# A new order of all steps of a one-core delta-rule and MLP kernel, and two of its last stores on another queue

## The chip, the cores and the metric

The kernel runs on one core of a Trainium2 chip. A core has five engines, each with its own queue of instructions that it takes strictly in order: TensorE (PE: matmuls, with the weight load PEld shown apart), VectorE (DVE), ScalarE (ACT), GpSimd (POOL) and SyncE (SP, which here only issues DMAs). The metric is the device time of one execution in microseconds. Before the change three runs gave 534.24, 536.07 and 537.71 us; the median is 536.07.

## The reference: what is computed

Two blocks in a row, all in 32-bit floats. The first is a delta-rule recurrence over 768 steps for 4 batches of 8 heads of width 48. Each head has a 48 x 48 state that starts at zero:

```python
k_n = k / (norm(k) + 1e-6)
for t in range(768):
    y[:, :, t] = q_t @ state
    v_old      = k_t @ state
    state     += beta_t * outer(k_t, v_t - v_old)
```

The eight heads' outputs of a token are put side by side, which gives x of 4 x 768 x 384. The second block works on each token:

```python
xn  = (x - mean) / sqrt(var + 1e-6) * g_ln
out = x + relu(xn @ w_ch1) @ w_ch2      # 384 -> 1536 -> 384
```

## The kernel before, in words

The 768 steps are cut into 12 chunks, c = 0 to 11, of C = 64 tokens. Inside a chunk the recurrence is solved with matrices; from chunk to chunk only the state is handed on. What one chunk goes through, with the names that the text uses:

- Loads of q, k and v (`load_raw`, `load_blocks`, `load_v`, all through `dma`, L407 to L411), and transposes into `kt` and `qt`.
- The gram matrix of the keys, G (`gram`, L843): 64 small matmuls of 48 x 64, a copy to `gsb` by ACT, and a store `gd` to DRAM by SP.
- The triangular inverse, `rows_inverse` (L874), called x0, x1, ... : SP loads the gram back as `gb` in another layout; ACT takes the root of its diagonal and DVE makes scales of it (`nrm_b`, `db_b`, L892 to L897); then DVE runs a chain of pairs, a multiply into `tmp` (L916) and a subtract from `xb` (L923), in which each pair needs the one before. The result goes to DRAM (`xd`) and comes back in yet another layout (`xt<-xd`, called xq in the steps' names). From x1 on one such inverse serves two chunks: x1 chunks 2 and 3, x2 chunks 4 and 5, and so on. The first two chunks have inverses of their own: chunk 0's `first_inverse`, and x0 with blocks of FB = 16 for chunk 1.
- `join`, which puts the blocks together on PE, and `queries`, the products P of queries and keys.
- `recur` (L1030), the recurrence itself: on PE the products with the old state (ks, qs), the solve (u), the output (y) and the state's update (s, L1114); on DVE the sums v (L1049) and `s_all` (L1124).
- The norm: statistics of x on DVE (L1148, L1149), `xln` (L1160), and a turn on PE (L1192) to `xnt`.
- `mlp(c)`: the two matmuls with relu between. Chunk 0 does them plainly (L1416, L1438); later chunks compute the second one by a scheme with 7 of 8 block products (`seven`, L1492), and from chunk 3 on the first one by a similar scheme (`fifteen`, L1283). Both replace matmuls by additions on DVE and POOL. The sums of the second one end on DVE and POOL (L1531).
- `put(c, g)` (L1455): the stores of the result, two DMAs for each half g of the chunk's tokens, four for a chunk, 48 in all.

**What sets the order.** The code does not issue instructions as it goes. Every call of `add` (L68) appends a *step* to a list: its engine, a function that issues its instructions, and the steps that it depends on. There are 3016 steps (a step of PE can hold 64 matmuls). At the end `Line.emit` (L90) plays them in the order of a long string of step numbers, `ORDER` (L131 to L254). The order is chosen once, offline; nothing is decided while the kernel runs. The costs, priorities and due times in the calls are for the search that made the string, and `emit` uses only one of them: a GpSimd step is made to wait for the newest DVE step before it that uses the port which both share. `in_this_order` (L25) ties the instructions of each engine to that order, the DMAs of SP's and ACT's queues too. So on each engine the order of the string is the order of execution, and between engines only the data dependencies count. The letter "f" in the string is a filler: one matmul of zeros into an unused part of bank `f_[0]` (`zeros`, L1590, two instructions in the profile), whose result nobody reads.

The steps that the text calls by number, so that they can be found in the string: 304 is the store of x0's result; 372 and 378 split weights into two halves on DVE (L598); 418 is a transpose and 442 the sum v of chunk 1; 447 is chunk 1's `s_all`; 457 its `xln`; 646 is the gram matrix G4; 861 and 920 are an output sum of the MLP of chunk 1 and v of chunk 3; 916 is the product P3; 2024 and 2036 are the stores of the gram matrices of chunks 10 and 11, which x5 reads; 2043 to 2046 are x5's four small scale steps; 1782 and 1800 are output sums of chunk 5's second matmul, 1812 a matmul that reuses the bank that 1800 reads; 3005, 3006, 3014 and 3015 are the last four stores.

Of the kernel before, what the change touches and what calls it, by code (L numbers as in the profile page):

```python
# [16 lines left out]
C = 64  # L17
# [114 lines left out]
53 9 54 8 47 0 10 76 52 1 11-12 5 13 57 35 39 4 79 55 48 59 61 36 58 49 66 37 80 56 38 43 62 40 75 6-7 65 71 86 257  # L132
89 63 85 96 90 41 91 24 18 97 42 81 44 98 2 23 64 73 26 99 15 21 92 87 82 69 83-84 14 88 33 100 50 402 105 101-102
74 93 104 94 30 95 72 17 106 20 19 124 107 103 108 118 70 109 16 125 77 110 226 119 111 27 29 32 31 112 126 128 120
f f f 133 127 123 130 325 121-122 67 78 129 404 238 113 215 326 114 131 134 406 115-116 132 22 234 f 135 117 316 216
141 136 34 137 147 144 140 209 403 145 138 411 142 139 143 146 407 148-149 214 222 68 151 150 228 210 264 240 157
265 211 154 262 155 25 153 232 315 28 227 156 212 266 229 162 313 152 248 159 f 163 414 158 230 165 164 260 160-161
314 166 51 168 244 167 263 174 170 259 220 169 261 239 173 180 176 241 327 171 175 172 181 409 45 177 183 246 217
245 410 182 178 184 328 179 250 258 413 f f 185 60 191 189 256 317 242 401 186-187 196 46 193 190 197 192 188 247
318 194 199 267 195 213 198 268 319 363 200-201 243 269 205 320 270-271 273 203 f 321 272 208 274 202 275-276 204  # L140
277 249 207 278 322 251 279-280 3 364 281 f f 329 282 206 283 224 284 638 337 285-286 323 339 287 331 324 330 340
288 332 650 342 289-290 370 338 333 469 344 291-292 235-236 341 293-294 369 295-296 334 297 347 335 298-300 252 223
336 348 301 405 231 302 343 225 408 218 f f f f f 361 303 237 304 352 254 353 412 345 640 362 253 652 346 354 477
415 f 435 349 233 365 350 359 475 434 255 219 351 367 309 366 308 360 437 368 f f 355 310 376 375 312 436 221 358 f
f f 438 311 399 356-357 306 382 575 416 307 439 642 305 470 577 641 474 576 473 476 579 578 639 371 417 440 373 381
581 372 377 767 374 580 614 379 378 583 418 387 380 442 419 584 388 766 478 587 479 420 480-481 582 482 485 585 769
588 394 484 400 486 421 487 586 488-489 393 654 490-491 385 615 492 637 771 493 422 383 591 768 644 494 764 651 495
389 423 589 649 496 592 497-498 424 499 590 656 500 772 501 643 502 770 503 763 595 504 428 505 426 773 506 395 507
593 390 425 508 427 596 509 429 510 441 511 433 512 431 645 432 616 430 397 599 513 1052 443 514 594 396 655 391 515
653 444 516 483 517 398 774 600 445 518 1054 908 601 907 446 448 447 519 1056 910 520 909 521 657 522 646 449 384  # L150
523 386 629 451 597 524 647 1055 525 452 392 526 450 648 527 453 1051 454 528 658 1064 1058 617 659 602 1066 598 660
603 455 912 765 458 456 529 618 459 530 619 531 1053 532 620 533 1057 621 534-535 604 661 665 605 536 460 662 606
537-538 663 607 630 608 539 457 609 540-541 664 610 542-544 775 545 631 546 461 547 776 465 548 622 902 467 466 611
623 913 462-463 900 624 464 468 625 666-667 778 668-670 550 626 672 777 1068 673 911 549 805 674-675 551 676-678 809
632 806 679 552 680 807 681 1158 682-683 633 613 811 808 1157 684 810 685 914 686 813 687 904 688-689 1159 690 815
1059 814 627 812 901 817 691 1526 905 553 1160 692 554 693 818 694 816 819 695 556 779 555 557-558 823 696 1528 820
697-698 559 471 824 699 821 829 560 832 700 562 915 830 561 1070 563 822 780 701 1063 1163 702 831 564 838 906 781
703 825 704-705 1530 706 839 784 707 1067 1164 634 1165 708 782 612 785 835 709 786 565 710 1525 787 840 836 711 841
788-789 842 791 833 843 1167 792 472 712 827 783 628 834 1156 713 916 671 714 1166 828 844 715 1162 826 793 855 569
903 716 848 567 837 717 849 1155 568 790 718 850 1069 566 856 719 794 1168 857 720 858 845 721 1169 859 722 851 1529  # L160
795 723 852-853 796 847 860 724 917 797 846 570 862 801 725 571 918 726 1532 798 727 802 728 1531 854 800 865 729
799 1527 866 730 804 873 731 803 732 1065 874 573 733 875 734 574 919 735 920 736 572 921 1170 867 922 861 1352 876
# [87 lines left out]
2907-2908 2930 2941 2909 2945 2942 2946 2967 2910 2943 2954 2947 2955 2948 2944 2956-2957 2933 2949 2958 2952 2934  # L250
2959 2968 2951 2960 2969 2935 2971 2961 2970 2972-2973 2962 2989 2981 2950 2974 2978 2975 2982 2953 2983 2990-2991
2963 2992 2984-2986 2993 2987 2976 2994 2988 2996 2995 2980 2997-2998 2979 2999-3001 3007 3002 3008 2977 3009 3003
3010 3004 3011-3012 3006 3013-3014 3005 3015
"""  # L254


# [1482 lines left out]
```

## Time and profile before

| | |
|---|---|
| runs | 534.24, 536.07, 537.71 us (median 536.07) |
| profiled execution | 533.75 us, span 532.0 us from first to last instruction |
| mean granted TensorE clock | 0.985 of full speed |
| instructions | 22724 |
| busy: PE, weight load | 497.6 us (94%), 451.9 us (85%) |
| busy: DVE, POOL, ACT | 366.4 us (69%), 281.3 us (53%), 207.9 us (39%) |
| moved by DMA | 54.56 MB, 181635 packets, most under 512 bytes |

The profile is of one execution. It gives the busy time of each engine, the same in 40 slices of the span (13.3 us each; a digit is the busy share in tenths, 9 means 90% or more), the granted clock of TensorE in the same slices, and the chain of work that ended last, followed back from the end. The trace behind it can be asked for windows (busy time of each engine in a stretch), for waits (what an engine waited for, by the line of the waiting instruction and the line of the one that released it), and for a timeline. Two instructions on one engine can overlap a little, as the start of the next is prepared while one ends.

### The profile page before, as it was taken

To read this page: it belongs to the slowest core of one execution; us is meant where nothing else is said; L and a number is where in the kernel's file an instruction comes from. 1 tells how busy PE (TensorE), PEld (TensorE's weight loads), DVE (VectorE), ACT (ScalarE), POOL (GpSimd) and SP (SyncE) were. 2 spreads that over 40 slices of the span, in tenths; PEclk is the share of its full clock that TensorE was granted. 3 is DMA by queue.
4 is the path that set the end of the run, shared out by engine and by line. 5 is a ranking of instruction groups with operands and counts; after the bars stand their busy time and mean duration, and the time that the engine had idled before them with its cause. 6 is when DMAs were issued, how large, how long until landed. Compare 5 with 4: busy or idle time off the path is not lost.

```text
span 532.0 us, 22724 instructions
## 1 busy us (share of the span) xinstructions
PE 497.6 (94%) x9942; PEld 451.9 (85%) x9942; DVE 366.4 (69%) x819; ACT 207.9 (39%) x451; POOL 281.3 (53%) x447
## 2 busy tenths in 40 slices
PE   5978798989989999999999999999999999999996
PEld 2766676758778888899999899999999999999996
DVE  3677748899996697994799982789985546244241
ACT  5677645412423332343342433442422623524130
POOL 6015574460573948757827617464266353554554
PEclk9789999999989999999999999999999999999999
DMA  9948798357635657156625157532435411212011
GB/s 174 289 73 194 178 207 160 78 111 139 119 58 120 150 115 123 34 141 154 100 65 97 21 135 198 116 70 33 101 74 104 91 31 37 56 40 53 1 30 31
DMA packets 181635, 54.56 MB, mean 103 GB/s; under 512 B 164888, under 2 KB 177312, under 8 KB 181536
## 3 DMA queue, kind: packets, MB, share of 16 engines
q1 hardware_dynamic: 168672, 40.30, 37.2%
q10 hardware_dynamic: 10656, 9.64, 6.6%
q0 software_dynamic: 2208, 3.17, 3.8%
q8 instruction: 78, 1.28, 1.0%
q14 instruction: 21, 0.17, 0.1%
HBM read 36.30 MB, written 16.78 MB: 100 GB/s over the span
## 4 chain that ended last, share of the span: by engine, by line
PE 67%; DVE 18%; issue 4%; ACT 2%; DMA 1%; POOL 1%; SPq 0%; ACTq 0%; DVEq 0%; POOLq 0%
PE f L1513 26%; PE f L1316 22%; DVE tmp L916 5%; PE f L1416 5%; DVE xb L923 4%; PE two L828 3%; PE by L1042 2%; PE two L1042 2%; PE by L1104 1%; PE two L1097 1%; DVE qt L923 1%; PE two L1114 1%; ACT xt L738 1%; DVE words L1488 1%; DVE st L1148 1%
## 5 line engine op out<-in xcount | busy, mean ns | idle before, releaser
L1513 PE MATMUL f<-w_sb,h_all 128*128 128x192 f32 x396 | 83.8, 331 | 1.8 <-issue 1.6
L1500 POOL TENSOR_TENSOR h_all<-h_all 128x256 f32<-128x256 f32 x99 | 73.9, 759 | 13.8 <-DVE tmp L916 6.3
L1513 PE MATMUL f<-words,h_all 128*128 128x192 f32 x396 | 80.0, 333 | 0.6 <-POOL h_all L1500 0.6
L1538 POOL TENSOR_TENSOR words<-h_all 128x128 f32<-128x128 f32 x66 | 30.3, 477 | 78.2 <-ACT h_all L1343 51.6
L1513 PEld LDWEIGHTS f<-words,h_all 128*128 128x128 f32 x396 | 66.0, 192 | 2.3 <-POOL h_all L1500 1.4
L1339 DVE TENSOR_TENSOR h_all<-f,h_all 128x512 f32<-128x512 f32 x72 | 48.8, 685 | 27.0 <-PE f L1316 22.0
L1513 PEld LDWEIGHTS f<-w_sb,h_all 128*128 128x128 f32 x396 | 65.7, 191 | 1.5 <-ACT words L1544 0.3
L916 DVE TENSOR_TENSOR tmp<-xb,gb 128x31 f32<-128x31 f32 (+19 forms) x139 | 60.2, 433 | 4.4 <-POOL xb L903 1.5
L923 DVE TENSOR_TENSOR xb<-xb,tmp 128x31 f32<-128x31 f32 (+19 forms) x139 | 55.5, 399 | 2.9
L410 POOL DMA_DIRECT2D tb<-in_k_dram x64 | 41.7, 655 | 20.5 <-DVE xb L923 9.3
L1416 PE MATMUL f<-xnt,w_sb 128*128 128x256 f32 x216 | 51.2, 384 | 0.0
L1334 ACT COPY h_all<-f 128x512 f32<-128x512 f32 x45 | 25.9, 586 | 61.6 <-PE f L1316 42.0
L1343 ACT ACTIVATE h_all<-h_all 128x512 f32<-128x512 f32 x54 | 32.9, 627 | 35.9 <-DVE h_all L1339 35.8
L1416 PEld LDWEIGHTS f<-xnt,w_sb 128*128 128x128 f32 x216 | 39.9, 190 | 7.3 <-issue 1.8
L1316 PE MATMUL f<-xnt,w_sb 128*128 128x128 f32 x288 | 41.1, 278 | 0.0
L1316 PE MATMUL f<-x_new,w_sb 128*128 128x128 f32 x288 | 40.7, 277 | 0.0
L1316 PEld LDWEIGHTS f<-x_new,w_sb 128*128 128x128 f32 x288 | 37.1, 191 | 0.4
L1316 PEld LDWEIGHTS f<-xnt,w_sb 128*128 128x128 f32 x288 | 36.7, 191 | 0.6
L611 POOL TENSOR_TENSOR w_sb<-words 128x768 uint32<-128x768 uint32 (+1 forms) x11 | 15.6, 1425 | 35.9 <-ACT xt L738 23.2
L1531 DVE TENSOR_TENSOR o<-f,x 128x192 f32<-128x192 f32 x33 | 11.3, 353 | 31.6 <-PE f L1513 29.1
L1142 ACT COPY x<-by 128x384 f32<-128x384 f32 x23 | 10.4, 480 | 43.8 <-DVE o L1531 28.1
L1425 ACT ACTIVATE h_all<-f 128x256 f32<-128x256 f32 x36 | 13.3, 380 | 36.0 <-PE f L1416 35.9
(252 smaller groups left out, 989.6 us busy)
## 6 DMA issues: line engine op xcount, KB each, us to landing
words<-in_moe_w_ch_dram ACTq DMA_DIRECT2D x20, 384.0 KB, 5.3
gd<-gsb SPq DMA_DIRECT2D x11, 512.0 KB, 3.1
v<-in_v_dram SPq DMA_DIRECT2D x24, 192.0 KB, 4.3
out_dram<-o SPq DMA_DIRECT2D x48, 96.0 KB, 2.3
kr<-in_k_dram SPq DMA_DIRECT2D x46, 96.0 KB, 3.7
xld<-xlt SPq DMA_DIRECT2D x9, 384.0 KB, 2.9
xnt<-xld SPq DMA_DIRECT2D x36, 96.0 KB, 2.8
tb<-in_q_dram SPq DMA_DIRECT2D x40, 64.0 KB, 3.2
```

The source lines that it names most:

```text
L410: add(eng, cost, lambda: QUEUE[eng].dma_start(out=out_, in_=in_), r, w, bulk=n * ns / 16e3, np=n, **kw)
L916: lambda j=j, n=n, w=w, t=t: nc.vector.tensor_tensor(out=t, in0=xv[:, 0:n, j : j + 1].to_broadcast([128, n, w]), in1=gv[:, j : j + 1, j + ...
L923: "DVE", dve(n * w), lambda t=t, rest=rest: nc.vector.tensor_tensor(out=rest, in0=rest, in1=t, op=ALU.subtract),
L1042: nc.tensor.matmul(dst[half(e), hp, j], src[drows(hp), (e if n else key_half(c, hp, e)) * GP + j], s_all[drows(hp), e, j], start=(n == 0 o ...
L1316: nc.tensor.matmul(wide(p[:, f : f + 128]), w[:, f : f + 128], r, start=start and i == 0, stop=True, skip_group_check=True)
L1334: add("ACT", act(512), lambda: nc.scalar.copy(o, p), pk, ok)
L1339: add("DVE", dve(512), lambda: nc.vector.tensor_tensor(out=o, in0=x, in1=y, op=op), [*xk_, *yk], ok)
L1343: add("ACT", act(512), lambda: nc.scalar.activation(o, o, ACTF.Relu, scale=scale), [], ok)
L1416: nc.tensor.matmul(p[:, 0:TOK], w1_sb[:, t, f * 128 : (f + 1) * 128], xnt[:, t], start=(t == 0), stop=(t == KC - 1))
L1500: add(eng, cost, lambda: e.tensor_tensor(out=out_, in0=x, in1=y, op=op), r, w, port=2 if eng == "Pool" else 1, pr=-2)
L1513: lambda f=f, t=start and f == order[0]: nc.tensor.matmul(p[:, 0:D2], lhs(f), rhs[:, f], start=t, stop=(f == order[-1]), skip_group_check=True
L1538: lambda f=f + i: e.tensor_tensor(out=s3[f], in0=one(0, 0)[0](f), in1=one(1, 0)[0](f), op=ALU.subtract),
```

## The change

Two edits. First, the string `ORDER` is replaced as a whole. The set of steps and their dependencies are the same; the new string comes from a new search, in which the time that each transfer takes was varied at random many times. It holds 15 fillers where the old one has 21. Seventy-three of the 3016 steps keep their place in the list; half of them move by 14 places or less, the farthest by 747. Second, in `put`, for the last chunk (c = 11), the store of the second pair of batches (e = 1) is issued from ACT's queue instead of SP's. These are the steps 3006 and 3015, one for each half g of the tokens.

```diff
 ORDER = """
-53 9 54 8 47 0 10 76 52 1 11-12 5 13 57 35 39 4 79 55 48 59 61 36 58 49 66 37 80 56 38 43 62 40 75 6-7 65 71 86 257
...
-3010 3004 3011-3012 3006 3013-3014 3005 3015
...
+2993-2994 2996-2997 2995 2998-3002 2979-2980 2988 3007-3013 3004 3003 3015 3006 3005 3014
 """
...
     def put(c, g):
         for e in range(2):
             dma(
-                "SP", out[2 * e + g, c * C : (c + 1) * C, :], os_[g][half(e)], C, 105, o_keys(g), [("out", c, g, e)], pr=-5
+                "ACT" if e and c == NCH - 1 else "SP", out[2 * e + g, c * C : (c + 1) * C, :], os_[g][half(e)], C, 105, o_keys(g), [("out", c, g, e)], pr=-5
             )
```

The new string is nine lines shorter, so every line of the kernel behind it has a number that is lower by nine after the change. What it does to the places that the text speaks of:

- At the start, three large fill matmuls stand behind the first transposes instead of ahead of them, and the loads of beta's rows come first on POOL. DVE takes x0's chain in among chunk 0's inverse. SP issues the store 304 directly behind a gram store.
- Steps 372, 378, 418 and 442, which DVE ran just ahead of x1's chain, stand inside it, and 861 and 920 move in among x1 and x2.
- ACT's root for x1 stands ahead of two relus of chunk 0's MLP.
- Steps 2043 to 2046 stand ahead of the sums 1782 and 1800 on DVE; on SP both gram stores 2024 and 2036 and x5's gb loads stand ahead of loads that were ahead of them.
- At the end SP's queue holds 3005 and then 3014, ACT's holds 3015 and then 3006.

## The prediction

> **What bounds the kernel now.** I read the page first: shares of engines, the span in slices, the chain that ended last.
>
> ```profile
> PE 497.6 (94%) x9942; PEld 451.9 (85%) x9942; DVE 366.4 (69%) x819; ACT 207.9 (39%) x451; POOL 281.3 (53%) x447
> ...
> PE   5978798989989999999999999999999999999996
> ...
> DVE  3677748899996697994799982789985546244241
> ...
> PEclk9789999999989999999999999999999999999999
> ...
> PE 67%; DVE 18%; issue 4%; ACT 2%; DMA 1%; POOL 1%; SPq 0%; ACTq 0%; DVEq 0%; POOLq 0%
> ```
>
> TensorE is busy for 94% of the span, so an order of the same instructions can win no more than its idle time: 532.0 − 497.6 = 34.4 us, and the slices put nearly all of that in the first half. The windows say how much is where, and what stands beside it (columns: span, then busy of PE, weight load, DVE, ACT, POOL, granted clock, DMA share, GB/s).
>
> ```profile
> 100.00:150.00 50.00, 44.76 (x936) 34.84 (x924) 47.69 (x103) 14.74 (x39) 22.00 (x32) 1.00 0.64 123
> 150.00:200.00 50.00, 47.39 (x1295) 42.16 (x1296) 38.39 (x84) 16.74 (x43) 30.59 (x40) 0.97 0.52 109
> 300.00:350.00 50.00, 49.94 (x1037) 48.13 (x1036) 34.36 (x79) 19.11 (x39) 22.77 (x40) 1.00 0.58 133
> ...
> 150.60:154.70 4.10, 4.06 (x72) 3.94 (x73) 3.93 (x12) 1.23 (x4) 1.49 (x3) 0.58 0.13 16
> ```
>
> From 100 to 150 us PE is idle 5.2 us while DVE is busy 47.7 of 50: DVE sets the pace there. It works off two inverses, x1 (DVE 78.79 to 121.35) and x2 (122.85 to 161.6), nearly without a gap, and what PE waits for stands behind them in DVE's queue. From 300 us PE has next to nothing to win and everything to lose. The chain's 18% of DVE is this first part. The waits of PE name the single stalls (total, times, longest):
>
> ```profile
> PE f L648 <- DMA u<-in_beta_dram: 2.6, 1, 2.6
> PE by L1192 <- DVE xln L1160: 2.6, 1, 2.6
> PE two L828 <- DVE s_all L1124: 2.2, 1, 2.2
> ```
>
> **The change part by part.** For each step I summed, with the durations of this execution, the work that stands ahead of it on its own engine in the old and in the new order. The difference says how much earlier or later its engine reaches it. It cannot say when its input is there, and that is where I chose.
>
> *Fillers.* 21 become 15.
>
> ```profile
> L1591 PE MATMUL f<-u 128*128 128x256 f32 x42 | 12.7, 432 | 0.0
> ```
>
> Two matmuls each: 12.7 / 21 = 0.60 us, six fewer is 3.6 us of PE busy time. They stand in the first 75 us, where PE idles 5.6 us of 0–13, 6.1 of 27–53 and 5.9 of 53–100, so I count 0 (bounds −3.6, if PE never waits where they stood, and +1.7, below). After PE had been busy 2.41 us of the 4.60 before 150.6, the clock was granted at half for 3.41 us (the 0.58 row above); one such stretch costs PE 3.41 / 2 = 1.7 us. The Trainium skill ("TensorE: Matmul & The Clock Gate", Part 1: The HAM clock gate) says that the array falls to half rate only after at least one idle window of about 3.4 us; no wait of PE here is longer than 2.6 us, and the clock fell all the same, so the trace is stricter than that rule; by the rule the missing fillers could cost nothing.
>
> *Start and x1.* The inverse x0 is moved forward among the first chunk's inverse on DVE. Its result's store, step 304, is what x1 waits for in the end (through the loads of xq, the gram store's queue and gb).
>
> ```profile
> 58.77 1.88 SPq L410 DMA_DIRECT2D beta_b<-in_beta_dram  x2
> 60.75 0.53 SPq L410 DMA_DIRECT2D xd<-xb  x1
> ...
> 65.38 6.05 SPq L410 DMA_DIRECT2D xt<-xd  x8
> 71.47 1.51 SPq L410 DMA_DIRECT2D gb<-gd  x2
> ```
>
> SP issued it 1.9 us after x0's last DVE step (58.83 to 60.75), behind two beta loads. In the new order these stand elsewhere, and from the store to the last gb load SP holds as much as before (12.2 against 12.4 us). So x1's chain starts 1.9 us earlier (bounds 0 and −6.2, the latter being SP's work less ahead of step 304). But four DVE steps that lay in DVE's idle time before x1 (8.3 us of it between 65 and 79 us) are now inside the chain: 372 (1.86), 378 (0.55), 418 (0.71), 442 (0.92), 4.04 us. With 861 and 920 also moved in, x1 and x2 together hold 88.3 us of DVE work against 83.0. At x2's end DVE is thus 5.3 − 1.9 = 3.4 us late before waits are counted; the gap between them (121.35 to 122.85) takes 1.3 of it, leaving 2.1.
>
> What PE sees of this, with PE's own work ahead (fillers off) against DVE's: G4 (646) needs chunk 1's state sum (447), which has 3.05 us more DVE work ahead while PE has 0.7 less: a new stall, 3.2 us. The L1192 wait grows by 0.3. The join of chunk 2 loses 0.7. The 2.2 us wait of P3 (916) goes, since PE has 2.27 us more work ahead of it and 4.9 when the fillers are left out; with it the idle time that came before the half clock at 151, 1.7 us. Sum: 3.2 + 0.3 − 0.7 − 2.2 − 1.7 = **−1.1 us** (bounds −6, when x1 starts 6 us earlier and the 3.2 goes, and +5.3, when it starts no earlier and all of DVE's extra work is paid).
>
> Late next, once these stalls go, is the recurrence at 205–235 us: DVE has 4 to 7 us more ahead of its steps there, but 12.8 us idle to take it, so 0. Without that cover it would be those 4 to 7 us, which I keep in the upper end.
>
> *Inverse x5 and chunk 5's sums.* In the new order the four small DVE steps that wait for x5's gb loads (2043 to 2046, 0.9 us) stand ahead of the sums 1782 and 1800 of the second matmul; before, they ran at 339.86 and the sums at 328.2. DVE takes its queue in order, and PE's step 1812 needs 1800 to have emptied its bank.
>
> ```profile
> 327.91 0.36 DVE L1531 TENSOR_TENSOR o<-f,words 128x192 f32<-128x192 f32 x1 [6.45 <-PE f L1513]
> ...
> 332.01 1.98 SPq L410 DMA_DIRECT2D gb<-gd  x2
> ...
> 335.20 1.09 SPq L410 DMA_DIRECT2D gb<-gd  x2
> ```
>
> The loads were issued late since the gram store 2024 stood behind xt loads until 327.85 although its data were there at 315.4. In the new order both gram stores stand ahead of these, the other one's data (320.26) being last; SP then holds 4.6 us to the end of the gb issues, 324.9, and from the last issue to the norm it took 3.3 us before (336.29 to 339.56): gb at 328.2, so the sums run about 1 us late. If instead SP is late as before, the loads gain only the 2.7 us that SP holds less between store and loads: 337.1 and 0.9 on top, 9.5 us late with everything of PE behind. I take **+2.0 us** (bounds 0 and +9.5), near the lower end, since the gram's data are long there.
>
> *The last stores.*
>
> ```profile
> 526.93 2.56 SPq L410 DMA_DIRECT2D out_dram<-o  x4
> 527.35 0.36 DVE L1531 TENSOR_TENSOR o<-f,o 128x192 f32<-128x192 f32 x1 [1.40 <-PE f L1513]
> ```
>
> SP issues all four: step 3006 at 526.93, 3014 at 527.74 (it waits for the last sum, done at 527.71), 3005 at 528.26, 3015 from 528.90 to 529.49; the last lands at 532.0. In the new order SP has 3005 and 3014, so it ends at 528.2, and ACT, idle there, has 3015 and then 3006. ACT takes its queue in order, so 3006, whose data are there at 526.91, stands behind 3015 and its wait for 527.71: with 0.37 to 0.50 us for one issue on ACT (its loads between 4 and 21 us) it ends at about 528.7. **−0.7 us** (bounds −1.3, if the landing follows SP's end, and 0, when transfers share engines so that the last one lands no earlier). The Trainium skill ("DMA: Bandwidth & Descriptors", Issuing engines are not separate DMA queues) says that issuing from several engines saves only the sequencer's time to issue; that time is what this term counts.
>
> Sum: 0 − 1.1 + 2.0 − 0.7 = +0.2 us on the profiled execution's 533.75 (span 532.0 and 1.75 around it), 533.9. That execution lies 2.3 us under the median of the runs, 536.07; on the median I forecast **536.3 us**.
>
> **Rivals.**
>
> *Slower: x5's norm blocks DVE at 328 us.* One mechanism: DVE's queue stands at step 2043 until gb lands, PE at 1812. Each microsecond that gb lands after 328.4 costs one, as PE has 0.06 us idle in that window. It passes 1% when the sums run about 7 us late (2.0 + 5.2), at 335.5. Full price 9.5 − 2.0 more than my sum: **543.8 us**. For it: some 20 loads and stores share SP from 316 to 336 us. Against: the stores are first there now.
>
> *Slower: x1 starts no earlier.* The four DVE steps are paid in full in a stretch that DVE paces, +5.3 instead of −1.1: **542.7 us**. For it: 47.69 of 50; against: 8.3 us of DVE's idle time before 79 us that an earlier chain can use.
>
> *Faster: the chain gets its 6.2 us.* If step 304 leaves by as much earlier as SP's queue allows, G4's new stall and the L1192 wait go, −6 instead of −1.1, 531.4 us, and the fillers' 3.6 us may come off the start's own path: **527.8 us**. For it: 29 us of PE's idle time lie before 300 us. Against: x0's own DVE chain must be that early.
>
> *The order moves nothing on the path.* PE's stalls only change places; the stores alone count: 536.07 − 0.7 = **535.4 us**.
>
> *Half clock.* If, with fewer fillers, two or three more stretches of 3.41 us at half clock follow, 1.7 us each: +3.4 to +5.1, about **540.5 us**.
>
> **How the numbers follow.** One per cent, 5.4 us, is about what a measurement of this kernel tells from no change. Chances: my sum 0.30, the order moving nothing 0.10, half clock 0.10 (three with the time within 1%, mostly), x5's block 0.13, x1 no earlier 0.10, the faster rival 0.27. The bounds of the terms spread each by some 3 us. Faster than 530.7: 0.27 — most of the faster rival and the low tail of my sum. Slower than 541.4: 0.28, from the two slower rivals and the high tails. Within: 0.45. The range 527 to 545 takes in both x5's full price and most of the faster rival; my sum's own range is 531 to 541.5.
>
> **What would show it.** Right: L1192 and L828 waits of PE change as told (2.2 gone, a new one at L828 behind s_all near 100 us); no 0.58 clock near 151; x1's first step at 76.9 instead of 78.8; the wait of DVE before the norm L893 near 328 about 1 to 3 us; last four stores in two queues, issued 0.7 us sooner after the last matmul. Wrong: PE's idle time from 300 us over 5 us, a wait of several microseconds on gb there, or x1's first step before 74 or after 80 us. What would make it wrong is a producer that moves later than the work ahead of it tells, most of all a DMA, since transfers' landing times under a new neighbourhood are in no sum of mine.

## The result, and the profile after

The changed kernel takes 554.51 us (median of four runs, 552.69 to 558.17); the kernel before took 536.89 us beside it (four runs). The ratio is 1.034 with a 95% interval of 1.0269 to 1.0411: 18 us slower. The forecast was 536.3 us, no change, with a range of 527 to 545; the result lies outside it.

The page of the changed kernel, of an execution of 552.69 us with a span of 550.9 us and a mean clock of 0.965 (engines; the slices of PE, DVE and the clock; the chain that ended last):

```profile
PE 500.1 (91%) x9930; PEld 456.0 (83%) x9930; DVE 375.8 (68%) x819; ACT 207.0 (38%) x451; POOL 284.2 (52%) x447
...
PE   3887699989899887699999999999999999999996
...
DVE  3567769899985489996499984698955436344141
...
PEclk9797799999899997989999999999999999999999
...
PE 60%; DVE 14%; DMA 4%; SPq 4%; issue 2%; ACT 1%; POOL 1%; DVEq 0%; ACTq 0%; POOLq 0%
```

PE's idle time, span less busy, grew from 34.4 to 50.8 us; its busy time grew by 2.5 us although six fillers are gone. Together that is the 18.9 us of the span. The clock's row has sevens in its slices 2, 4, 5 and 16 (13.8 us each, so 14 to 28, 41 to 69 and 207 to 220 us) and eights in 11 and 18. From the 19th on it is full, as before: the second half lost nothing.

To place the loss I took, in both traces, the moment at which PE had done the same amount of its work (without fillers). The new kernel is 5.7 us behind at 70 us of the old one's time, 4.5 at 196, 11.7 at 208, 16.6 at 220, 18.2 at 231, and then 17 to 20 to the end. Between the first two the lag falls to about 3 us near 110 and rises to 7 or 8 near 140; as the two orders differ, each figure holds to some 2 us. So there are two places: **the start**, and **the stretch from 200 to 240 us**, where some 14 us go. The windows of the second one, first of the kernel before, then of the changed one (span, busy of PE, weight load, DVE, ACT, POOL, clock, DMA share, GB/s):

```profile
205.00:210.00 5.00, 5.00 (x33) 5.00 (x32) 2.57 (x5) 1.95 (x5) 3.57 (x5) 1.00 0.70 112
230.00:235.00 5.00, 5.00 (x98) 4.75 (x98) 4.48 (x8) 1.89 (x4) 3.64 (x7) 1.00 0.85 264
```

```profile
205.00:210.00 5.00, 0.00 (x0) 0.00 (x0) 4.59 (x14) 0.10 (x1) 0.00 (x0) 0.85 0.17 30
210.00:215.00 5.00, 4.48 (x72) 4.39 (x73) 4.72 (x10) 0.80 (x1) 2.80 (x4) 0.50 0.03 7
...
230.00:235.00 5.00, 1.37 (x48) 1.27 (x40) 4.97 (x6) 0.80 (x2) 4.11 (x5) 0.74 0.07 10
235.00:240.00 5.00, 5.00 (x24) 5.00 (x24) 4.38 (x11) 0.89 (x4) 2.65 (x3) 0.58 0.05 7
...
100.00:150.00 50.00, 44.61 (x890) 34.02 (x890) 45.84 (x95) 16.94 (x40) 22.41 (x30) 0.97 0.50 99
150.00:200.00 50.00, 47.63 (x1188) 41.99 (x1188) 33.83 (x75) 18.28 (x47) 24.39 (x35) 1.00 0.61 123
300.00:350.00 50.00, 48.46 (x968) 46.80 (x968) 36.60 (x76) 15.81 (x33) 32.14 (x51) 1.00 0.63 124
```

Twice PE stands still, and twice the clock is then granted at about half for some 7 us. The three wide windows, in which the prediction looked for gains and losses, moved by 1.5 us of PE's busy time at most. PE's waits in the changed kernel say what it stood for (total, times, longest; line numbers are nine lower than before):

```profile
PE f L639 <- POOL ident L421: 8.3, 1, 8.3
PE two L1088 <- DVE v L1040: 6.3, 1, 6.3
PE f L1504 <- DVE o L1522: 4.7, 2, 3.6
PE f L1582 <- DVE u L1074: 4.5, 1, 4.5
...
PE by L1183 <- DVE xln L1151: 2.4, 3, 1.5
```

The 8.3 for `ident` is not lost as such: before, PE filled that time with its fill matmuls, and its first transposes of keys started at 7.26 us, where they start at 8.60 now.

The 6.3 is the recurrence of chunk 4 (u4), which waits for its sum v, step 1175 on DVE. That step runs at 209.52 us; before, it ran at 183.5. Its two inputs come later too: PE's product ks4 ends at 194.8 instead of 182.5, and POOL's step 1161 moved from 171.5 to 199.7. POOL's timeline shows what happened to 1161 (start, duration, line, operation; in brackets the idle time ahead):

```profile
180.67 1.14 POOL L1522 TENSOR_TENSOR o<-o,words 128x192 f32<-128x192 f32 x2
194.74 1.29 POOL L894 COPY xb<-db_b 128x32 f32<-128x32 f32 x1 [12.92 <-DVE db_b L888]
195.96 0.45 POOL L1529 TENSOR_TENSOR words<-h_all 128x128 f32<-128x128 f32 x1
196.35 0.66 POOL L401 DMA_DIRECT2D tb<-in_k_dram  x1
197.02 0.88 POOL L1529 TENSOR_TENSOR words<-h_all 128x128 f32<-128x128 f32 x2
197.84 1.27 POOL L1267 TENSOR_TENSOR w_more<-w_more,w_sb 128x512 f32<-128x512 f32 x1
199.05 0.66 POOL L401 DMA_DIRECT2D tb<-in_k_dram  x1
199.72 1.49 POOL L682 TENSOR_TENSOR v<-v,kpair 128x768 f32<-128x768 f32 x1
201.15 0.87 POOL L1529 TENSOR_TENSOR words<-h_all 128x128 f32<-128x128 f32 x2
201.98 0.72 POOL L1491 TENSOR_TENSOR h_all<-h_all 128x256 f32<-128x256 f32 x1
202.66 1.26 POOL L1267 TENSOR_TENSOR pt<-pt,w_sb 128x512 f32<-128x512 f32 x1
```

The copy at 194.74 is step 1086, which puts the scales of x3's diagonal into `xb`. It waits for x3's norm. In the new order 1161 (the L682 row) and others stand behind it, fifteen steps with 12 us of work by the durations of before, that stood ahead of it there (950, 955, 980 to 985, 1161, 1350, 1525, 1531, 1532, 1537, 1540). Ten of them had their inputs by 182.6 us; the loads for 1161 had all been issued by 155.2. POOL takes its queue in order, so it idles 12.92 us and then does most of this work in one run. That run meets x3's chain on DVE, of which step 1090 is one. In the kernel before, then in the changed one, where the last row is v of chunk 4:

```profile
192.70 0.22 DVE L916 TENSOR_TENSOR tmp<-xb,gb 128x60 f32<-128x60 f32 x1
```

```profile
196.49 0.47 DVE L914 TENSOR_TENSOR xb<-xb,tmp 128x31 f32<-128x31 f32 x1
196.99 7.01 DVE L907 TENSOR_TENSOR tmp<-xb,gb 128x60 f32<-128x60 f32 x1
204.04 0.22 DVE L914 TENSOR_TENSOR xb<-xb,tmp 128x60 f32<-128x60 f32 x1
...
209.52 0.95 DVE L1040 TENSOR_TENSOR v<-v,two 128x768 f32<-128x768 f32 x1
```

Step 1090, a multiply of 128 x 60 that takes 0.22 us before, takes 7.01 us: it begins with POOL's run of nine instructions at 197.02 and ends with it, at 204.00 against 203.92. What stands behind it on DVE, v of chunk 4 among it, is late by that much. When v starts, 1161 has been done for 8 us (201.21) and DVE has had no idle time just ahead: in the end v waits for its place in DVE's queue, behind x3's steps, and not for 1161.

### The profile page after: what moved, and what is told of

Its sections match the earlier page's. It is cut to its first block, busy times and chain, and to the rows that moved or that the text cites. A ratio compares the mean times of both kernels' runs of the same rounds, so it can differ in the third digit from the quotient of the medians.

```text
span 550.9 us, 22698 instructions
## 1 busy us (share of the span) xinstructions
PE 500.1 (91%) x9930; PEld 456.0 (83%) x9930; DVE 375.8 (68%) x819; ACT 207.0 (38%) x451; POOL 284.2 (52%) x447
## 4 chain that ended last, share of the span: by engine, by line
PE 60%; DVE 14%; DMA 4%; SPq 4%; issue 2%; ACT 1%; POOL 1%; DVEq 0%; ACTq 0%; POOLq 0%
PE f L1504 21%; PE f L1307 19%; PE f L1407 7%; DVE tmp L907 5%; SPq L401 4%; DVE xb L914 3%; PE two L819 2%; PE two L1088 2%; PE by L1095 2%; PE two L1033 1%; PE by L1033 1%; DMA xld<-xlt 1%; PE two L1105 1%; DMA xnt<-xld 1%; DVE qt L914 1%
## 5 line engine op out<-in xcount | busy, mean ns | idle before, releaser
L1504 PE MATMUL f<-w_sb,h_all 128*128 128x192 f32 x396 | 85.7, 335 | 7.8 <-DVE o L1522 3.6
L907 DVE TENSOR_TENSOR tmp<-xb,gb 128x31 f32<-128x31 f32 (+19 forms) x139 | 69.1, 497 | 4.5 <-POOL xb L894 1.2
L914 DVE TENSOR_TENSOR xb<-xb,tmp 128x31 f32<-128x31 f32 (+19 forms) x139 | 60.9, 438 | 3.0
L1407 PEld LDWEIGHTS f<-xnt,w_sb 128*128 128x128 f32 x216 | 41.1, 195 | 9.5 <-issue 2.1
L1522 DVE TENSOR_TENSOR o<-f,x 128x192 f32<-128x192 f32 x33 | 11.5, 350 | 43.5 <-PE f L1504 38.5
L1307 PE MATMUL f<-xnt,w_sb 128*128 128x128 f32 x288 | 39.9, 279 | 0.0
L1307 PEld LDWEIGHTS f<-xnt,w_sb 128*128 128x128 f32 x288 | 36.9, 194 | 0.3
L1504 PE MATMUL f<-w_sb,words 128*128 128x192 f32 x132 | 27.7, 329 | 1.1 <-DVE o L1522 1.1
L1416 ACT ACTIVATE h_all<-f 128x256 f32<-128x256 f32 x36 | 13.3, 382 | 31.5 <-PE f L1407 30.7
```

What stands on the lines that cost most here:

```text
L907: lambda j=j, n=n, w=w, t=t: nc.vector.tensor_tensor(out=t, in0=xv[:, 0:n, j : j + 1].to_broadcast([128, n, w]), in1=gv[:, j : j + 1, j + ...
L914: "DVE", dve(n * w), lambda t=t, rest=rest: nc.vector.tensor_tensor(out=rest, in0=rest, in1=t, op=ALU.subtract),
L1307: nc.tensor.matmul(wide(p[:, f : f + 128]), w[:, f : f + 128], r, start=start and i == 0, stop=True, skip_group_check=True)
L1407: nc.tensor.matmul(p[:, 0:TOK], w1_sb[:, t, f * 128 : (f + 1) * 128], xnt[:, t], start=(t == 0), stop=(t == KC - 1))
L1416: lambda hk=hk, p=p: nc.scalar.activation(h_all[:, hk] if c <= LNPE else h_all[:, hk].rearrange("p (g i b) -> p i g b", g=2, b=BK), p[:, 0 ...
L1504: lambda f=f, t=start and f == order[0]: nc.tensor.matmul(p[:, 0:D2], lhs(f), rhs[:, f], start=t, stop=(f == order[-1]), skip_group_check=True
```

## The experiments

All experiments change only the string `ORDER` (and the stores, where said), so the work is the whole of the reference's. Intervals are 95%; a percentage times the some 536 us of the kernel before gives the microseconds.

**Which part of the order (h1, h2, h3).** Two hybrids, cut at step 1060, the gram matrix G6 (near 150 us).

```diff
 ORDER = """
-(old string)
+(new string up to 1060; then the steps left, in the old string's order)
```

> The new order up to and with step 1060 (gram G6, 173.0 us in the new profile, 169.7 in the old), then all steps left over in the old order, stores on SP. Theory 'region': of the 18 us, 3 to 4 are lost before G6 and 14 behind it, between 200 and 240 us, by the new order of POOL and DVE around x3 and chunk 4. Then this kernel is 2 to 5 us slower than the old one, about 540, c4's sum v (1175) is no more than 5 us later than in the old profile (183.5), and DVE's step 1090 takes its 0.2 us. Theory 'start': the new start makes x3's gram loads late, and everything behind follows from that; then this one is 12 to 18 us slower, about 552. Theory 'spread': the loss is all over; then about 545.

Measured: 543.32 against 536.86 us, 1.0114 (1.0075 to 1.0153), +6.1 us.

```diff
 ORDER = """
-(old string)
+(old string up to 1060; then the steps left, in the new string's order)
```

> The old order up to and with step 1060, then all steps left over in the new order, last stores in two queues. Theory 'region': 12 to 15 us slower than the old kernel, about 550, with POOL idle for about 10 us ahead of x3's copy (1086), one DVE step of x3 that takes several us, and PE waiting 4 us or more at u4 (1176) for v. Theory 'start': within 4 us of the old kernel, about 538. Theory 'spread': about 545.

Measured: 548.82 us, 1.0232 (1.0178 to 1.0285), +12.5 us. The two add up to 18.6 us, the whole loss being 18.2: two separate causes, and the larger one lies behind G6. In h2's trace POOL's run holds x3's step of 128 x 87 for 4.82 us, and PE waits 5.3 us for v of chunk 4, as in the full change.

A third hybrid takes the new order only to step 361, s of chunk 0.

```diff
 ORDER = """
-(old string)
+(new string up to 361; then the steps left, in the old string's order)
```

> The new order only up to and with step 361 (chunk 0's state, 67.0 us in the new profile, 60.0 in the old), then all steps left over in the old order, stores on SP. The new order up to G6 (173 us) with the old rest cost 1.1%, 6 us. Theory 'start': chunk 0's u and state come 7 us later, since DVE runs x0's chain among chunk 0's inverse, and x1, x2 and what follows inherit it: 4 to 7 us slower than the old kernel (0.8 to 1.3%). Rival 'middle': DVE makes up for the start while it waits for x1, and the loss is made by the order between 67 and 173 us: under 2 us slower (under 0.4%).

Measured: 541.03 against 534.84 us, 1.0107 (1.0061 to 1.0152), +5.7 us. The new start with the old rest thus costs as much as the whole first part (h1). It is not quite the start of the change, though: x1's norm comes at 87.7 us in h3, at 76.2 in h1 and at 77.4 in the changed kernel. That the first part is lost in the first 70 us is read from the lag of 5.7 us there; what x1 and x2, which the prediction argued over, add to it or give back, these runs do not tell apart.

**POOL's queue behind 1086 (e2, e8a, e10, e6).** In the changed kernel four of the delayed POOL steps go back ahead of 1086.

```diff
-888 892 ... 943 980 1531 981 983 950 1540 1161 984 982 986 1087 955 1088
+888 980 950 1161 955 892 ... 943 1531 981 983 1540 984 982 986 1087 1088
```

> The new order with four POOL steps (980, 950, 1161, 955; 4.5 us of work), whose inputs are there by 180 us, taken from behind x3's copy 1086 to ahead of it (behind 888), into POOL's 12.9 us of waiting. Nothing moves on DVE. Theory 'run on POOL holds DVE': in the new profile DVE's step 1090 took 7.01 us (0.22 elsewhere) and ended when POOL's run of additions (195.96 to 203.92) ended; with 4.5 us less in the run it takes about 2.5, v of chunk 4 (1175) comes 4.5 us earlier, PE's wait of 6.3 us at u4 falls to 2 or less, and the kernel gains 4 to 8 us (with some half clock), about 548. Rival 'place in DVE's queue': v is late since 25 steps of x3 stand ahead of it, not for 1090's length; then 1090 stays above 5 us, and the kernel gains under 2 us, about 553. Third: DVE's step 1090 waits for something else that the profile does not show (its length unchanged at 7).

Measured: 549.52 against 536.86 us, 1.0226 (1.0186 to 1.0267): 12.1 us over the kernel before where the change has 18.2, so four moved steps bring 6 back. The step that took 7.01 us takes 0.53.

Then twelve steps.

```diff
-888 892 ... 963 926 ... 959 938 ... 943 980 1531 981 983 950 1540 1161 984 982 986 1087 955 1088
+888 1525 1531 1532 1161 980 950 955 1537 1540 892 ... 963 983 926 ... 959 981 982 938 ... 943 984 986 1087 1088
```

> The new order with twelve POOL steps taken from behind x3's copy 1086 to ahead of it, as they stood in the old order: 1161, 980, 950, 955, 983, 981, 982 and the transfers 1525, 1531, 1532, 1537, 1540, 9.6 us of POOL's time by the old profile. POOL waited 12.9 us ahead of 1086 in the new profile with all of them behind it. Only POOL's order changes. Theory 'POOL's queue': DVE's steps 1090 (7.01) and 1130 (4.27) fall under 1.5 us each, v of chunk 4 comes some 6 us earlier, PE's waits at u4 (6.3) and at 1042 (3.6) fall under 2 us, and 9 to 13 us come back: 542 to 546. Rival 'order on DVE and PE': v (1175) still stands behind 25 steps of x3 on DVE, and the gain is that of four POOL steps moved, 5 us: about 549.5, with idle time and half clock left between 215 and 240 us.

Measured: 543.78 against 534.21 us, 1.0186 (1.014 to 1.0231): 9.9 us over, so 8 us of the 18 come back, less than the 9 to 13 expected. The wait of u4 is gone; step 1090 takes 0.22 us again, and 1130 takes 1.64.

The same move in h2, where the start is the old one:

```diff
-888 892 ... 963 926 ... 959 938 ... 943 980 981 983 950 1540 1161 984 982 986 1087 955 1088
+888 1161 980 950 955 1537 1540 892 ... 963 983 926 ... 959 981 982 938 ... 943 984 986 1087 1088
```

> The old order up to G6, then the new order with nine POOL steps (1161, 980, 950, 955, 1537, 1540, 983, 981, 982) ahead of x3's copy 1086, where the old order had them; without that move it was 2.3% slower than the old kernel, 12.5 us. Theory 'POOL's queue, apart from the start': the move brings 8 us back here as it did behind the new start, leaving 3 to 5 us (0.6 to 1.0%). Rival 'the two meet': behind the old start x3 comes in time and the move brings all back, within 2 us of the old kernel; or little, as DVE's order is what counts here, more than 8 us slower.

Measured: 543.34 against 534.84 us, 1.0143 (1.0093 to 1.0193): 7.6 us left of 12.5. The move is worth some 5 us without the new start, and it does not return everything.

The reverse, in the kernel before: eleven POOL steps that stood ahead of 1086 are put directly behind it.

```diff
-... 1082 985 1348 ... 1177 1086 1351 1088-1090
+... 1082 1348 ... 1177 1086 950 980 955 983 981 984 982 985 1540 1537 1350 1351 1088-1090
```

> The reverse, in the old kernel: eleven POOL steps (950, 980, 955, 983, 981, 984, 982, 985, 1540, 1537, 1350; 8.6 us by the old profile) taken from ahead of x3's copy 1086 to directly behind it. No other engine's order changes. Theory 'a run on POOL holds DVE': behind 1086 POOL has 8 us of additions without a wait, and x3's first DVE steps, 0.2 us each in the old profile, last together 4 us or more longer, one of them 3 us at least; chunk 4's state sum (1179) comes 4 us later, and the kernel is 4 to 9 us slower, 541 to 546. Rival 'POOL's place is harmless, it is DVE's own order that is late': DVE's steps keep their 0.2 to 0.4 us and the time stays within 2 us, unless PE waits for the additions themselves (then a wait of m2's matmuls on POOL shows).

Measured: 540.45 against 534.21 us, 1.0115 (1.007 to 1.0159), +6.2 us. This makes the slowdown in the old order by POOL's queue alone. DVE and POOL in this run:

```profile
193.81 1.20 DVE L915 TENSOR_TENSOR tmp<-xb,gb 128x31 f32<-128x31 f32 x1 [0.41 <-POOL xb L902]
...
198.88 2.74 DVE L915 TENSOR_TENSOR tmp<-xb,gb 128x135 f32<-128x135 f32 x1
```

```profile
193.70 1.26 POOL L1275 TENSOR_TENSOR w_more<-w_more,w_sb 128x512 f32<-128x512 f32 x1
...
203.18 1.36 POOL L1275 TENSOR_TENSOR w_sb<-w_sb 128x512 f32<-128x512 f32 x1 [1.73 <-DVE tmp L915]
```

Steps of x3 that took 0.19 and 0.30 us take 1.20 and 2.74 while POOL runs, and step 1179, DVE's sum of chunk 4's state, ends up 6.9 us later (199.4 to 206.3). PE pays in another place than in the changed kernel: 3.78 us at 210.74 for POOL's sum 996, itself queued behind the late run.

**POOL's steps made to wait for DVE's (e11).** Here each engine keeps the changed kernel's order of its own; ten POOL steps only move in the string behind pairs of x3, so that `emit` gives each of them a wait for the newest DVE step on the shared port. In the new string these steps stand in a bunch behind 943, ahead of DVE's 1088, so none of them waited for x3's pairs.

```diff
-943 980 1531 981 983 950 1540 1161 984 982 986 1087 955 1088-1106
+943 1087-1089 980 1531 1090-1091 981 1092-1093 983 1094-1095 950 1540 1096-1097 1161 1098-1099 984 ...
```

> The new kernel with every engine's own order unchanged. Ten POOL steps stand directly behind x3's copy 1086 and ahead of x3's first DVE step 1088 in the string, so that POOL runs through them without a wait on DVE; here they are put behind 1089, 1091, 1093 and so on to 1105, one for two DVE steps, so that each POOL step waits for the DVE step ahead of it, and nothing else changes. Theory 'a run on POOL without a pause holds DVE': step 1090 falls from 7.01 to under 1.6 us, with several DVE steps of 0.6 to 1.6 us after it, and v (1175) comes 2 to 5 us earlier; the time is 0 to 5 us better, 549 to 554. Rival 'DVE waits for something else at 1090': it still takes over 4 us, and the time is the same or worse by the waits added.

Measured: 551.25 against 534.84 us, 1.0299 (1.0248 to 1.0349). The 7.01 us step is gone; the longest of the next pairs are these:

```profile
200.16 1.25 DVE L915 TENSOR_TENSOR xb<-xb,tmp 128x135 f32<-128x135 f32 x1
...
201.80 1.75 DVE L915 TENSOR_TENSOR xb<-xb,tmp 128x156 f32<-128x156 f32 x1
```

Step 1130, further on and not reached by these moves, still takes 4.28 us. PE's wait for v falls from 6.3 to 3.1 us. The time falls by some 2 us, less than the intervals can tell. So waits let DVE in between; but POOL's work stays behind 1086, and most of the loss stays with it. The stretched step is not what most of the time went to.

**Repairing the named wait alone (e3).** In the changed kernel 1161 goes behind 888 on POOL, and v (1175) ahead of x3's first step on DVE.

```diff
-888 892 ... 939 1081 ... 1540 1161 984 ... 1106 1175 1107
+888 1161 892 ... 939 1175 1081 ... 1540 984 ... 1106 1107
```

> The new order with only chunk 4's two v steps moved: POOL's 1161 ahead of x3's copy (behind 888) and DVE's sum 1175 ahead of x3's first DVE step 1081. Theory 'region', with v as the path: PE does not wait at u4 any more (6.3 us before), no half clock near 210, gain 7 to 10 us, about 546, though DVE's step 1090 still takes 4 us or more, since most of POOL's run is left. Rival 'the chain of x3 is the path': x3's chain is as late as before and PE waits as long a little later (chunk 5's sums), gain under 3 us, about 552.

Measured: 556.04 against 536.86 us, 1.0341 (1.03 to 1.0382): nothing gained. The wait of 6.3 us is gone, and PE waits all the same:

```profile
218.83 0.59 PE L1504 MATMUL f<-words,h_all 128*128 128x192 f32 x2 [2.91 <-POOL h_all L1491]
...
222.73 4.30 PE L1504 MATMUL f<-words,h_all 128*128 128x192 f32 x14 [2.22 <-DVE o L1522]
...
229.56 0.59 PE L1504 MATMUL f<-w_sb,words 128*128 128x192 f32 x2 [1.38 <-DVE o L1522]
```

The two last rows wait for output sums on DVE, the first for POOL: with one step earlier, the next one that DVE or POOL has late is waited for.

**More of DVE's order put back (e8b, e13).** On top of the twelve POOL steps, chunk 4's steps on DVE go earlier.

```diff
-741 886 ... 742 927 ... 958 897 ... 952 939 ... 1106 1175 1107
+741 1172 886 ... 742 1173 927 ... 958 1175 897 ... 952 1533 939 ... 1106 1107
```

> As the kernel with twelve POOL steps moved, and besides on DVE and PE the steps of chunk 4's start as early as in the old order: the mask of P4 (1172) ahead of chunk 3's norm, ks4 (1173) directly behind e4 on PE, v (1175) ahead of the sum 897, and the keys' transpose 1533 ahead of 939. Theory 'POOL's queue': within 2 us of the kernel with POOL's steps alone. Rival 'order on DVE and PE': 5 to 8 us better than that one, 541 to 544, near the loss of the start alone (the new start with the old rest: 543.3).

Measured: 546.89 against 534.21 us, 1.0248 (1.0205 to 1.0291): 3 us worse than without. PE takes 1173 in its order too and waits 2.29 us for 1172 there.

Or, in h2 with the POOL move, the sums of chunk 3's MLP go between the pairs of x3.

```diff
-1005 1118 1119 ... 1122 1360 1123 1012 ... 1126 1022 1127
+1005 ... 1179 1118 1360 1012 1119 1022 1120-1123 ... 1126 1127
```

> The kernel with the old order up to G6, then the new one with nine POOL steps moved (1.4% slower than the old one, 7.6 us), and on DVE three sums on which PE waited moved ahead of x3's pairs: 1179 (chunk 4's state) directly behind 1005, 1012 behind 1118, 1022 behind 1119. Theory 'DVE's queue': PE's waits of 1.5 us at P5 (1360) and 1.4 us at 1031 go, and with them the half clock at 222 to 226 (1.7 us): 3 to 5 us less, 0.5 to 0.9% slower than the old kernel. Rival: x3's pairs are then later by the same and PE waits at the next sums (1030, 1042) or at v of chunk 5; gain under 1.5 us.

Measured: 545.02 against 534.55 us, 1.0179 (1.0128 to 1.023): no gain over 1.0143. The waits at 1360 and 1031 are gone, new ones stand at 1362 (1.19) and 1042 (2.26).

**The start (s1, e14).** With the new start alone (as in h3), DVE's chunk-0 steps go back ahead of x0's pairs.

```diff
-274 275 217 247 ... 278 193 279 280 281 192 282 ... 287 198 200 ... 301 340 302 338 303
+217 247 193 192 274 ... 279 197 199 330 650 198 280 281 200 282 ... 340 ... 338 ... 303
```

> The kernel with the new order up to step 361 and the old rest (1.1% slower than the old one, 5.7 us), with chunk 0's DVE steps taken out from behind x0's pairs: 193 and 192 ahead of 274, 198 behind 279, 200 behind 281, u's 340 behind 289 and 338 behind 291, on PE 199 directly behind 197, and four fillers put behind 333. Theory 'x0 on DVE holds chunk 0': u (338), done at 64.05 in the new profile and 54.85 in the old, comes by 58, and 3 to 6 us come back, 0 to 0.5% slower than the old kernel. Rival 'the start's other changes' (transfers, fills, POOL): u comes late all the same or the gain is under 1.5 us.

Measured: 539.0 against 534.55 us, 1.0092 (1.006 to 1.0123). The gain on 1.0107 is under 1 us and inside the intervals. Chunk 0's u came only 4.1 us earlier (done at 61.4 us instead of h3's 65.5).

All three repairs in the changed kernel, POOL's twelve steps, the sums and the start:

```diff
-(e8a's string)
+(e8a's string with the moves of the two diffs above)
```

> The new kernel with all repairs: twelve POOL steps ahead of 1086, chunk 0's DVE steps as in the start's repair, and the three DVE sums. If the three causes add up: 18 less 8 (POOL, measured), 3 to 6 (start) and 3 to 5 (sums): 0 to 4 us slower than the old kernel (0 to 0.8%). If it stays over 8 us slower (1.5%), a cause is missing.

Measured: 543.17 against 534.55 us, 1.017 (1.012 to 1.022), no better than the POOL move alone within the intervals.

**The stores alone (e7)**, in the kernel before: the second edit and the new order of the last four.

```diff
-3012 3006 3013-3014 3005 3015
+3012 3013 3015 3006 3005 3014
...
-                "SP", out[2 * e + g, ...
+                "ACT" if e and c == NCH - 1 else "SP", out[2 * e + g, ...
```

> The old kernel with the second edit alone: stores 3006 and 3015 on ACT's queue and the last four stores in the new order (3015, 3006 on ACT; 3005, 3014 on SP). From the prediction: the last issue ends at about 528.7 instead of 529.49, 0.7 us less, about 536.2, not to be told from 0 by the times but in the trace, where the stretch from PE's last matmul (527.25) to the end (532.0) should fall from 4.75 to about 4.0 us. Rival: the transfers' landing sets the end, and the stretch stays at 4.7 or grows.

Measured: 533.41 against 534.21 us, 0.999 (0.9963 to 1.0016). The tail of this run:

```profile
524.17 1.27 SPq L409 DMA_DIRECT2D out_dram<-o  x2
524.59 0.36 DVE L1530 TENSOR_TENSOR o<-f,o 128x192 f32<-128x192 f32 x1 [1.40 <-PE f L1512]
524.98 1.38 ACTq L409 DMA_DIRECT2D out_dram<-o  x2
```

From PE's last matmul to the end of the span it takes 4.5 us here and in the changed kernel, where it took 4.8: 0.2 to 0.3 us.

**A version that beats both.** The kernel before with the second edit, the stores 3005 and 3006 ahead of the last sum, and the second load of beta's rows (65) directly behind the first on POOL.

```diff
-66 37 ... 7 65 71
+66 65 37 ... 7 71
...
-3012 3006 3013-3014 3005 3015
+3012 3005 3006 3013-3014 3015
```

> The old kernel with the second edit, its last stores in the order 3005 (SP) and 3006 (ACT) ahead of the last sum, 3014 (SP) and 3015 (ACT) behind it, and the load of beta's second rows (65) moved on POOL from behind ident to directly behind 66. Expected: the last two stores issue at once after the last sum, so that PE's end to the span's end falls from 4.75 to 4.0 us; PE's wait for the load (2.6 us at 13.5 us) falls under 1 us, of which DVE's later waits may take all. 0 to 3 us faster than the old kernel. Rival: nothing but the stores' 0.2 to 0.7 us is left, not to be told from 0.

Measured: 531.79 against 534.84 us, 0.9944 (0.992 to 0.9969): 3 us faster than the kernel before, and by the two ratios (0.9944 / 1.034) 3.8% faster than the changed one. PE's wait of 2.6 us for beta is not among this run's waits; one of 1.9 for `ident` stands in place of one of 1.3. By the trace, the stretch from PE's last matmul to the end is 3.9 us in this run, 0.9 less than before and some 0.6 less than in e7: by these traces the order of the last four stores is worth more than the second queue. Otherwise what each part is worth was not measured apart, but for e7's −0.8 us of the medians, which is inside its interval.

On top of it, two DVE steps of chunk 1's norm and the state sum of chunk 2 ahead of the pairs that delay them:

```diff
-531 532 ... 539 457 609 ... 710 ... 783
+531 ... 457 532-536 537 ... 710 ... 783 787 711 788-789 791-792 712
```

> The old kernel with the second edit, the stores' order and beta's load moved (0.6% faster than the old one), and DVE's steps 460 and 457 (chunk 1's norm) put directly behind 531 in x1's chain, 783 (chunk 2's state sum) behind 710 in x2's. PE's waits of 2.6 to 3.2 us at L1192 and 1.1 to 2.2 us at P3 (916), both on DVE steps that stood ready for 4 us or more behind pairs of an inverse, should go, and the half clock behind them: 3 to 6 us more, 1.1 to 1.7% faster than the old kernel. Rival: DVE sets the pace there, PE waits as long at the next step that needs x1 or x2, and the gain over the kernel without the move is under 1 us.

Measured: 532.76 against 534.55 us, 0.9967 (0.9945 to 0.999). PE's waits for `xln` and for P3 are gone and a new one of 2.7 us for chunk 2's `pt` has come: no gain over the version above.

## Why the prediction was wrong, step by step

- **What bounds the kernel** was read rightly: the first half has the idle time, from 300 us PE has nothing to lose. The lag stays within 17 to 20 us from 240 us to the end.
- **The step that failed most** is the sentence "the recurrence at 205–235 us: DVE has 4 to 7 us more ahead of its steps there, but 12.8 us idle to take it, so 0". That is the place where 14 us were lost. Three things in it failed.
  - The cover was not there. From 205 to 235 us DVE was busy 25.96 of 30 us before the change, so 4.0 us were idle and not 12.8. What idle time DVE has lies ahead of that stretch, and the new order leaves it unused: from 150 to 200 us DVE idles 16.2 us (11.6 before), and v of chunk 4 stands behind x3's steps, the first of which DVE starts at 193.65, after 2.50 us of waiting for ACT.
  - The step on which PE then waited longest, v of chunk 4 (1175), stood ahead of that stretch, at 183.5 us. Summed as the prediction sums, with the durations of the execution before, it has 13.3 us more DVE work ahead of it in the new order, chunk 4's state sum (1179) 10.0, and POOL's 1161 has 11.5 us more POOL work, not 4 to 7.
  - The sum takes a step's place in its own engine's queue and, as the prediction says itself, "cannot say when its input is there". Between 180 and 195 us a POOL step with a late input, 1086, holds up ready work; the run behind it then holds up DVE's steps in turn. POOL's queue was not looked at.

  What the runs show in place of 0: h2, which has the new order from G6 on, measures +12.5 us, and the kept upper end, 4 to 7 us, was too small as well. POOL's queue behind 1086 is worth 8 us of the loss in the changed kernel (e8a), some 5 in h2 (e10), and +6.2 us when it is made in the old order (e6).
- **The start** was taken as a gain ("x1's chain starts 1.9 us earlier"). x0's pairs moved forward on DVE, and x1's norm does come earlier (78.8 to 77.4 us). But what they were moved past was not costed: chunk 0's steps 198 and 200 (L776 below), on which chunk 0's u depends. In the kernel before, then in the changed one:

```profile
44.16 0.74 DVE L785 COPY_PREDICATED pt<-u,two 128x512 f32<-128x512 int32 x1 [0.23 <-PE two L780]
45.31 0.73 DVE L785 COPY_PREDICATED pt<-u,by 128x512 f32<-128x512 int32 x1
```

```profile
50.50 1.40 DVE L907 TENSOR_TENSOR tmp<-xb,gb 128x39 f32<-128x39 f32 x1
...
54.49 0.72 DVE L776 COPY_PREDICATED pt<-u,two 128x512 f32<-128x512 int32 x1
55.10 0.71 DVE L776 COPY_PREDICATED pt<-u,by 128x512 f32<-128x512 int32 x1
```

  They run 10 us later, u ends at 64.1 instead of 54.9, and PE's 4.5 us wait for u is the start's largest besides `ident`. x0 itself ends later, not earlier (58.8 to 64.1). h3 prices the start at +5.7 us against a term that was to be a small gain. That the late steps 198 and 200 make it is only argued: s1, which moves them back, gained no more than 1 us. One reading was wrong besides: the gap between x1 and x2, which was to take 1.3 us, was no idle time; DVE was busy for all 1.50 us from 121.35 to 122.85.
- **Fillers at 0.** Six fillers fewer gained nothing, and by windows of 2 us the clock is low at 20 to 28, 44 to 52 and 60 to 70 us, where before it was low at 14 to 22 and 28 to 32. What this low clock adds to the start was not measured, but the start costs as much without it: in h1, with the same new start, the mean clock of the first 75 us is 0.93, as before (0.86 in the changed kernel), and h1 is 6.1 us slower all the same.
- **Half clock.** The rival's mechanism was real, its price too low. By windows of 2 us, the clock time lost up to 400 us grew from 6.8 to 18.8 us. This counts time in which PE stood idle too, and the stretches at 140, 208 and 232 us each follow a wait of PE or begin in one; it adds to the price of the waits and can't be taken as 12 us of its own.
- **G4, L1192, P3.** The P3 wait of 2.2 is gone, as told. The `xln` wait is 2.4 in place of 2.6 + 0.3. The clock near 151 is full, as told. G4 runs 5.6 us later with no stall of its own: it shares the start's lag. The term of −1.1 can't be measured apart from that lag; h1 less h3 is +0.4, but x1 runs 11 us later in h3.
- **x5's norm**, the likeliest slower rival, did not come about. ACT's root is done at 342.7 us and DVE takes it at 347.04, behind a sum that waited for PE. The term +2.0 measured at most 1: the lag at 357 us is 19.4, at 324 us 18.5.
- **The last stores.** −0.7 was mis-sized; 0.2 to 0.3 us are saved. ACT's two issues took 0.55 and 0.73 us, not the 0.37 to 0.50 of its loads at the start.
- **The chances.** 0.28 on slower was split between two mechanisms: x5 cost at most 1 us, and what x1 cost can't be told apart from the start. The third, one engine's queue standing behind a wait for another, was known for SP and DVE and not looked for on POOL.

*What stays open.* Of the start's 5.7 us no single step was found. Of the 12.5 us behind G6 the POOL move returns 4.8 with the old start (7.6 remain) and 8 in the changed kernel, where 9.9 remain with the start's 5.7 among them. In the traces of e8a and e10 PE then waits for DVE near 220 us: 1.70 us for chunk 4's state sum and 1.37 for an output sum in e8a, 1.53 and 1.38 in e10, each time with one stretch of 3.41 us at half clock behind it (1.7 us), together some 4.7 us. But e13, which moves these sums forward, only met other waits, and why DVE is late there was not settled. In the same traces PE also stands 1.7 to 2.5 us near 184 us without a releaser that the profile shows; the kernel before has such a stall too, 1.65 us at 200.5, so little of the rest can lie in it, but for the half clock behind it in e10 (another 1.7 us).

## What to carry to other kernels

When a queue is reordered, list for every engine the steps that now stand behind a step with a late input, and ask what else waits on them: here 12 us of POOL's work, most of it ready, stood behind one small copy. Idle time of an engine covers extra work only if the engine can reach that work before the wait, and if no other engine holds what it needs. And a repair of the longest wait in the list moves it when the engine behind it is late as a whole; five such repairs (e3, e8b, e13, s1, best2) gained nothing that can be told, while moving ready work into an idle engine's gap gained 5 to 8 us (e2, e8a, e10).

## What the runs showed of the hardware

**A short DVE instruction can wait through a whole run of POOL's.** Step 1090 waited 7.01 us through nine POOL instructions, eight of them on tensors; step 1130 of the same inverse took 4.27 us where it takes 0.39, and in e6 0.30 became 2.74. The Trainium skill ("SBUF — State Buffer", SBUF: two separate sides) says that VectorE and GpSimd share a pair of ports as an exclusive lock, held for the whole instruction, and that the other one then fully blocks. The traces agree that one blocks the other. By the lock for one instruction alone, the wait would end with POOL's first, 0.5 us here; the measured one went through all nine. Where POOL's steps were made to wait for DVE's (e11), the longest of those pairs took 1.75 us, while step 1130, which these moves did not reach, still took 4.28.

**Half clock after short waits.** In e10 the clock is granted at 0.7 from 184 and at 0.5 from 186 to 188 us; the only long wait of PE just ahead is the 2.48 us of this row:

```profile
184.73 3.19 PE L1507 MATMUL f<-w_sb,h_all 128*128 128x192 f32 x9 [2.48 <-issue]
```

In the changed kernel it is 0.56 and 0.59 from 140 to 144 us behind a wait of 3.03. In the waits of 6.30 (204.2 to 210.5) and 3.63 us (230.7 to 234.3) the clock is still full from 206 to 208 and from 230 to 232 us, then 0.63 from 208 to 210 and 0.60 from 232 to 234. If it falls from full to half in these windows, it falls near 208.5, 4.3 us into the first wait, and near 232.4, only 1.7 us into the second. The first agrees with the Trainium skill's one idle window of about 3.4 us ("TensorE: Matmul & The Clock Gate", Part 1: The HAM clock gate); the second, and those behind waits of 2.48 and 3.03, do not reach it, as the one in the prediction did not.
